# An attention and SwiGLU training kernel: weight gradients on 20 full row tiles, with transposes moved between TensorE and the DMA crossbar

## The chip, the cores and the metric

The kernel runs on one core of a Trainium2 chip. The metric is device time in microseconds (us) for one launch, the median of several runs. A core has TensorE (matrix products, results in PSUM), VectorE, ScalarE and GpSimd for work on tiles, SyncE, which here only issues DMAs, and 16 DMA engines that all queues share. Each engine runs its instructions in order; DMAs are issued from SyncE's queue (SP), ScalarE's and GpSimd's. A transposing DMA ("crossbar transpose") turns rows into columns on the way into SBUF.

## The reference

The launch computes the output and all gradients of a block on x of 2048 rows by 640, in bf16:

```
xn  = layernorm(x)
s   = memory attention over 64 segments of 32 rows, one after the other:
        h = [mem (8 rows); xn segment (32 rows)]        40 rows
        q, k, v = h Wq, h Wk, h Wv                      32 heads of 128
        p = softmax(mask(q k^T / sqrt(128)))
        o = (p v) Wo;  mem = o[first 8 rows];  s rows = o[last 32 rows]
g   = silu( (silu(xn w1) * (xn w3)) w2 )                F = 1728
out = x + s * g
gradients of x, mem0, Wq, Wk, Wv, Wo, w1, w3, w2 for a given grad_out
```

Because each segment's memory comes from the one before, h has 2048 + 64 x 8 = 2560 rows in all: 2048 x rows and 512 memory rows.

## The kernel before

The stages follow each other: layer norm and SwiGLU forward (to about 450 us), attention forward, attention backward (the chain over segments, to 3394 us), weight gradients (`phase6_Awgrads`, 3394 to 4905), the gradient of Wo (`phase6b_gWo`, to 5085) and SwiGLU backward with the layer norm's (`phase5_Bbwd_ln`, to 5535).

Attention works on tiles `tl` of three segments, 22 in all: 21 with 120 rows (24 memory rows first, then 96 x rows) and one of 40. `geo(tl)` gives segments, memory rows nm, x rows nx and all rows n. Probabilities P and score gradients dS of a tile are stored in DRAM as `PR[tl]` and `DSR[tl]`, n rows by 32 heads by n columns; inputs and row gradients lie in stores that `x_src`, `m_src` and `g_src` address.

The weight-gradient stage takes eight blocks `qd` of 4 heads (512 columns) and in each the 22 tiles; a unit `u` is one tile in one block. For each unit:

- `ld` loads dS, P and three row tiles `r6` (the gradient of o, q and k): four loads on SP for dS, P and the x rows of q and k, one on ScalarE's queue, the memory rows on GpSimd's.
- `s1` transposes dS on TensorE (4 heads, L1333) and VectorE copies it out (L1335).
- `s2` makes the rows' gradients of v, k and q (L1345, 12 products), which ScalarE and VectorE copy to `gr` (L1348 to L1352); 22 tiles stay for the whole block.
- `s3` transposes `gr` on TensorE (12 products, L1364), and copies put it into `ring`, a cyclic buffer of 384 rows.
- `s4` multiplies each complete window of 128 rows of the ring by the transposed weights (L1381, 24 products) and adds it to `ghacc`, the gradient of h (L1388, L1390). It does so for all 2560 rows, 20 windows, although only x rows are read later.

After the 22 units, `wg` makes the three weight gradients of the block (L1403): for each, 5 sums over the 22 tiles, and stores them through SP (L1408). `ld_w` loads the block's weights by crossbar transposes, and the generator `head` puts the first units of the next block between the three `wg`. `in_order` ties the instructions of the stage on every engine to the written order, so no engine takes a later unit's instruction first.

`turned_load` (L280) issues a crossbar transpose on SP. Besides the weights, the SwiGLU backward uses it for gz (16 transposes), for ggT (112) and for `GU`, the stored up gradient. Its matrix products are `pghb` (L1757), `pgxb` (L1773), `w2a` (L1726) and `wa` (L1809). This stage is not held to the written order.

Of the kernel before, what the change touches and what calls it, by code (L numbers as in the profile page):

```python
# [16 lines left out]
P = 128  # L17
# [23 lines left out]
class K:  # L41
# [76 lines left out]
    def build_masks(self, pool, scr):  # L118
        nc = self.nc
        GE = ALU.is_ge  # L120
        n, nm = 120, 24
# [7 lines left out]
        for (c0, w) in ((0, 8), (nm, 32)):  # L129
            v1 = a1[:, c0:c0 + 3 * w].rearrange("p (s c) -> p s c", c=w)  # L130
            v2 = a2[:, c0:c0 + 3 * w].rearrange("p (s c) -> p s c", c=w)
            sel(v1, 1, 0, [[-8, 3], [0, w]])
            sel(v1, -1, 7, [[8, 3], [0, w]])
            sel(v2, 1, -nm, [[-32, 3], [0 if w == 8 else -1, w]])
            sel(v2, -1, nm + 31, [[32, 3], [0, w]])
# [8 lines left out]
        sel(b1[:], -1, 7, [[0, 40]])  # L144
        sel(b2[:], 1, 0, [[-1, 40]])
# [6 lines left out]
    def setup_dram(self):  # L152
# [17 lines left out]
        self.GXA = mk("GXA", (self.NR, D))  # L170
# [23 lines left out]
        for tl in range(self.NTL):  # L194
            n = self.geo(tl)[3]
            self.PR.append(mk(f"PR{tl}", (n, H, n)))
            self.DSR.append(mk(f"DSR{tl}", (n, H, n)))
            ns, nm = self.geo(tl)[0:2]
            self.VTD.append(mk(f"VTD{tl}", (P, ns, H, 40)))
        self.PM = mk("PM", (T, P, 80))  # L200

# [25 lines left out]
    def m_src(self, tl, w, c0, c1):  # L227
        g = c0 // 1024
        out, t = [], 3 * tl
        end = t + self.geo(tl)[0]  # L230
        while t < end:
            e = min(end, t - t % 4 + 4)
            XS = self.store(w)[t // 4, g, 0:8, t % 4:t % 4 + e - t]
            for i in range(2 if w == "qv" else 1):
                X = XS[:, :, i] if w == "qv" else XS
                out.append((8 * (t - 3 * tl), 8 * (e - 3 * tl), X[:, :, c0 - 1024 * g:c1 - 1024 * g].rearrange("r t c -> t r c"), i))
# [8 lines left out]
    def m_rows(self, A, t):  # L245
        r = 120 * (t // 3) + 8 * (t % 3)
        return A[r:r + 8, :]

    def x_rows(self, A, X, eng):
        n = self.NTL - 1  # L250
        eng.dma_start(A[0:120 * n, :].rearrange("(t r) d -> t r d", r=120)[:, 24:120],
                      X[0:96 * n, :].rearrange("(t r) d -> t r d", r=96))
        eng.dma_start(A[120 * n + 8:self.NR, :], X[96 * n:self.S, :])


    def x_pieces(self, A, x0, x1):
        out, a = [], x0
        while a < x1:
            tl = a // 96
            b = min(x1, 96 * tl + 96)  # L260
            r = 120 * tl + self.geo(tl)[1] + a - 96 * tl
            out.append((a - x0, b - x0, A[r:r + b - a, :]))
            a = b
        return out
# [103 lines left out]
def phase3_Afwd(k, W4, Wv, Wk_):  # L368
# [30 lines left out]
    with tc.tile_pool(name="ast", bufs=1) as st, tc.tile_pool(name="achain", bufs=1) as ch, \  # L399
# [174 lines left out]
        def ld(w, tl, qd, eng=nc.sync):  # L574
# [4 lines left out]
            k.load_x(r, nm, k.x_src(tl, w, c0, c0 + 512), eng)  # L579
# [11 lines left out]
        def scores(tl, qd):  # L591
# [8 lines left out]
            for j in range(4):  # L600
                kv = kT[:, h0 + j, 0:n].rearrange("p (s c) -> p s c", c=40)
                nc.tensor.matmul(sp[:, j, 0:nm], qT[:, j, :], kv[:, :, 0:8], start=False, stop=True,
                                 skip_group_check=True)
                nc.tensor.matmul(sp[:, j, nm:n], qT[:, j, :], kv[:, :, 8:40], start=False, stop=True,
# [19 lines left out]
        def norm(tl, qd, eng=nc.gpsimd, q=nc.gpsimd):  # L624
# [6 lines left out]
            q.dma_start(k.PR[tl][:, h0:h0 + 4, :], Pb[0:n, :, 0:n])  # L631
# [19 lines left out]
        def pv(tl, qd, q=nc.gpsimd):  # L651
# [3 lines left out]
            if 4 * tl < k.NO:  # L655
                pt = ps.tile([P, 4, 96], F32, name="xot", tag="x", bufs=5)
                for j in range(4):
                    nc.tensor.matmul(pt[:, j, :], v[0:n, j * P:(j + 1) * P], PTs[qd % 2][0:n, j, 24:120], start=True, stop=True)
# [126 lines left out]
def phase3b_out(k, Wo, W0, W4):  # L785
# [12 lines left out]
    with tc.tile_pool(name="oio", bufs=1) as io, tc.tile_pool(name="oac", bufs=1, space=bass.MemoryType.PSUM) as pa, \  # L798
# [6 lines left out]
        def ld(b, qd):  # L805
# [3 lines left out]
            if nt == 3:  # L809
                src = k.OR[120 * tl:120 * tl + 360, c0:c0 + 512].rearrange("(t r) c -> r t c", r=120)[24:120]  # L810
            else:
                nm, n = k.geo(tl)[1], k.geo(tl)[3]
                src = k.OR[120 * tl + nm:120 * tl + n, c0:c0 + 512].rearrange("(t r) c -> r t c", t=1)
# [82 lines left out]
        while g0:  # L896
# [6 lines left out]
    later = [(k.GWO[0:120 * n, :].rearrange("(t r) d -> t r d", r=120)[:, 24:120], k.GS[0:96 * n, :].rearrange("(t r) d -> t r d", r=96)),  # L903
             (k.GWO[120 * n + 8:k.NR, :], k.GS[96 * n:k.S, :])]

    for s in range(3):
# [3 lines left out]
        for b in range(2):  # L910
            r0 = 120 * tl0 + 8 * s
            dst = k.HRO[120 * tl0:120 * tl0 + 120 * (n - 1), :].rearrange("(t r) d -> t r d", r=120)[:, 8 * s:8 * s + 8]
            r1 = 120 * (tl0 + n - 1) + 8 * s
# [3 lines left out]
            later.append((k.HRO[r1:r1 + 8, cols], k.FS[t1, 32 * b:32 * b + 8, :]))  # L917
# [6 lines left out]
def phase4_Abwd(k, out2, WoT, WvT, WkT, WqT, later):  # L924
# [3 lines left out]
    with tc.tile_pool(name="gst", bufs=1) as st, tc.tile_pool(name="gchain", bufs=1) as ch, \  # L928
# [6 lines left out]
        bdf = st.tile([P, 16, 8], BF16, name="bdf")  # L935
# [338 lines left out]
def phase6_Awgrads(k, X, out0, out3, out4, out5):  # L1274
# [6 lines left out]
    R = 384  # L1281
# [618 lines left out]
```

## Time and profile before

| what | us |
|---|---|
| median of 3 runs | 5541.81 (5536.53 to 5544.77) |
| profiled execution, its own time | 5536.53 |
| its span, first to last instruction | 5534.8 |
| TensorE busy in the span | 4889.1 (88%) |
| VectorE, ScalarE, GpSimd busy | 2323.4, 1746.8, 1583.1 |
| weight-gradient stage, 3394 to 4905 | TensorE busy 1410.89 of 1511, granted clock 0.96, DMA share 0.44 |
| w2 gradient, 5085 to 5175 | TensorE busy 68.95 of 90 |
| SwiGLU backward with layer norm, 5175 to 5412 | TensorE busy 208.38 of 237, VectorE 125.28, DMA share 0.73 |
| w1 and w3 gradients, 5412 to 5535 | TensorE busy 117.33 of 123 |

All but the first row are of one profiled execution. Matmuls are pipelined, so their listed durations overlap and a busy engine can still take more. A queue's instructions (SPq) are listed with the time that they hold the queue, not with the time to landing.

### The profile page before, as it was taken

The page shows a single profiled execution, that of the slowest core. Times are in us where ns is not written, and L with a number is a line of the kernel's source. Part 1 is how long each engine was busy: PE and PEld are TensorE (multiplying, and loading weights), DVE is VectorE, ACT ScalarE, POOL GpSimd, SP SyncE. Part 2 cuts the span into 40 slices and gives each one's busy share as a digit, 9 for nine tenths or more (in the row PEclk, how much of TensorE's full clock was granted, in tenths as well). Part 3 has the DMA queues.
Part 4 walks back from the last instruction along what each step waited for, and adds up shares of the span by engine and source line. Part 5 has one row for each costly group of instructions (what it writes and reads, how often), then busy time and mean ns, then how long its engine had stood idle before and what let it go on. Part 6 is the DMA issues. An engine that isn't in the chain of part 4 may idle for free. (4 is left out here: it accounts for less than half of the span.)

```text
span 5534.8 us, 164066 instructions
## 1 busy us (share of the span) xinstructions
PE 4889.1 (88%) x66145; PEld 3115.9 (56%) x66492; DVE 2323.4 (42%) x7358; ACT 1746.8 (32%) x4913; POOL 1583.1 (29%) x2620
## 2 busy tenths in 40 slices
PE   4987888888888676989999996999999999998899
PEld 2544555555555444656666664566566556656555
DVE  5833555555555323444444542233223323311351
ACT  2422555555555322323333331232223222300000
POOL 0000344444444212333333333243224323310110
PEclk9998999999999787999999998999999999999999
DMA  7553455555555686666766665354335334548573
GB/s 251 172 186 90 138 158 151 156 151 161 153 149 143 147 178 148 181 187 183 191 183 182 185 175 124 89 122 102 83 89 122 93 84 97 130 163 226 130 161 95
DMA packets 1193943, 817.94 MB, mean 148 GB/s; under 512 B 742603, under 2 KB 1086311, under 8 KB 1190507
## 3 DMA queue, kind: packets, MB, share of 16 engines
q1 hardware_dynamic: 952451, 564.78, 39.1%
q0 software_dynamic: 93520, 151.54, 9.8%
q10 hardware_dynamic: 147212, 91.09, 6.5%
q8 instruction: 525, 8.60, 0.7%
q14 instruction: 235, 1.93, 0.1%
HBM read 461.39 MB, written 296.78 MB: 137 GB/s over the span
## 5 line engine op out<-in xcount | busy, mean ns | idle before, releaser
L1403 PE MATMUL wg<-gr,hr 120*128 120x512 bf16 (+1 forms) x2640 | 591.1, 385 | 17.3 <-DVE dST L1335 13.1
L1381 PE MATMUL g<-w,gT 128*128 128x320 bf16 x3840 | 549.9, 300 | 0.0
L1403 PEld LDWEIGHTS <-hr 120*128 120x128 bf16 (+1 forms) x2640 | 258.3, 99 | 342.0 <-issue 50.1
L1381 PEld LDWEIGHTS <-gT 128*128 128x128 bf16 x3840 | 369.3, 98 | 137.4
L243 POOL DMA_DIRECT2D r<-GOS x256 | 143.3, 564 | 796.2 <-PE r6p L1345 706.5
L90 DVE CAST wgo<-wg 128x512 bf16<-128x512 f32 x72 | 47.5, 688 | 585.9 <-issue 280.2
L316 PEld LDWEIGHTS <-hx 128*32 128x32 bf16 x7680 | 180.4, 98 | 169.7 <-issue 13.7
L90 DVE CAST stg<-bank 128x512 bf16<-128x512 f32 x256 | 177.1, 692 | 209.2 <-PE bank L316 199.6
L335 PEld LDWEIGHTS <-gkv 128*8 128x8 bf16 x8192 | 190.0, 87 | 105.7 <-DVE gkv L1012 24.2
L619 ACT ACTIVATE xP<-xsp,xnm 120x120 bf16<-120x120 f32 (+1 forms) x704 | 239.9, 375 | 8.8 <-DVE xnm L615 5.0
L1390 DVE TENSOR_TENSOR ghacc<-ghacc,g 128x320 f32<-128x320 f32 x240 | 117.2, 488 | 277.6 <-PE g L1381 277.6
L92 ACT CAST wgo<-wg 128x512 bf16<-128x512 f32 x48 | 25.8, 589 | 638.6 <-PE wg L1403 638.6
L1163 POOL DMA_DIRECT2D DSR<-gdS x176 | 101.5, 577 | 429.5 <-DVE gdS L1161 384.1
L1348 ACT CAST gr<-r6p 120x512 bf16<-120x512 f32 (+1 forms) x176 | 103.1, 586 | 362.4 <-PE r6p L1345 340.7
L668 POOL DMA_DIRECT2D OR<-xv x163 | 94.5, 580 | 420.0 <-ACT xv L667 304.1
L92 ACT COPY gT<-t6g 128x960 bf16<-128x960 bf16 (+5 forms) x216 | 166.9, 792 | 120.2 <-PE t6g L1364 117.4
L630 POOL TENSOR_TENSOR xP<-xP,xrz 120x480 bf16<-120x480 bf16 x163 | 161.7, 992 | 141.1 <-ACT xP L619 96.5
L1161 DVE SCALAR_TENSOR_TENSOR gdS<-gdp,Dx,gPr 120x120 bf16<-120x120 f32 (+1 forms) x680 | 182.8, 330 | 0.0
L1232 PE MATMUL gbank<-WqT,ident 128*128 128x512 bf16 x453 | 158.0, 398 | 20.0 <-issue 12.3
L1364 PE MATMUL t6g<-ident,gr 120*128 120x120 bf16 (+1 forms) x2112 | 172.0, 221 | 3.3 <-DVE wgo L90 2.7
L316 PE MATMUL gbank<-WoT,gox 128*32 128x512 bf16 x2560 | 153.7, 387 | 23.8 <-POOL gox L967 20.5
L335 PE MATMUL bank<-Wo,oTm 128*32 128x320 bf16 x4032 | 172.6, 324 | 0.1
(329 smaller groups left out, 10835.2 us busy)
## 6 DMA issues: line engine op xcount, KB each, us to landing
QVS<-stg SPq DMA_DIRECT2D x128, 256.0 KB
gqv<-QVS SPq DMA_DIRECT2D x108, 192.0 KB
vTt<-VTD SPq DMA_DIRECT2D x64, 320.0 KB
VTD<-gvT POOLq DMA_DIRECT2D x168, 120.0 KB, 3.7
OR<-xv POOLq DMA_DIRECT2D x163, 120.0 KB, 2.5
DSR<-gdS POOLq DMA_DIRECT2D x168, 112.5 KB, 3.4
dS<-DSR SPq DMA_DIRECT2D x168, 112.5 KB
P<-PR SPq DMA_DIRECT2D x168, 112.5 KB
```

Source lines behind the costliest of these rows:

```text
L90: return nc.vector.tensor_copy(out, in_)
L92: return nc.scalar.copy(out, in_)
L243: eng.dma_start(d, src if src.shape[0] > 1 else src[0])
L316: k.nc.tensor.matmul(bank[32 * g:32 * g + 32, :], x[:, dc, :], W[:, dc, c0:c0 + 512], start=(dc == 0), stop=(dc == k.DC - 1), tile_positio ...
L335: k.nc.tensor.matmul(pm[p0:p0 + nq, 0:320], x[:, h, :], W[:, h, 320 * b:320 * b + 320], start=(first and i == 0), stop=(last and i == 15), ...
L619: nc.scalar.activation(Pb[0:n, j, 0:n], sp[0:n, j, :], ACT.Exp, bias=nmx[0:n, j:j + 1], scale=k.scale, accum_out=Z[0:n, j:j + 1])
L630: eng.tensor_tensor(Pb[0:n, :, 0:n], Pb[0:n, :, 0:n], bc_last(rz[0:n], n), ALU.mult)
L1161: nc.vector.scalar_tensor_tensor(dS[0:n, j, :], dp[0:n, j, :], Dx[0:n, j:j + 1], Pr[0:n, j, :], op0=ALU.subtract, op1=ALU.mult)
L1232: nc.tensor.matmul((bA if g in ("W1", "G1", "G2") else bB)[:], k.ident[:], WqT[:, 0, 0:512], start=True, stop=True)
L1364: nc.tensor.transpose(pt[:, i - i0, j, :], st["g", u, i][0:n, j * P:(j + 1) * P], k.ident[0:n, 0:n])
L1381: nc.tensor.matmul(pg[:], ring[:, i, j, r0:r0 + P], Ws[qd][i][:, j, 320 * h:320 * h + 320], start=(i == 0 and j == 0), stop=(i == 2 and j ...
L1403: nc.tensor.matmul(accs[dc][:], hr[0:n, tl, dc * P:(dc + 1) * P], st["g", NTL * qd + tl, i][0:n, :], start=(tl == 0), stop=(tl == NTL - 1))
```

## The change

- In every tile x rows now come first and memory rows last; masks, slices and stores follow. P and dS are stored with 128 columns per head in place of n, the unused ones zero.
- The ring and the products of `s4` take x rows alone: 16 windows instead of 20. Two partial tiles (`NF` = 20 and 21) come first in each block and have ring rows of their own.
- `wg` sums over 20 tiles of 128 rows: the 160 rows of the two partial tiles go to DRAM (`GSP`) and come back as rows 120 to 127 of the 20 full tiles (`spill`). `hr` is loaded in the same way.
- dS is transposed by a crossbar transpose (`dturn`), and so are the x rows of `gr` into the ring (`s3`): four per unit on SP in place of 16 TensorE transposes and their copies. Loads run 5 units ahead.
- In the SwiGLU backward it is the other way: gz, ggT and guT are transposed on TensorE and copied out of PSUM, with fewer PSUM buffers for the products; `GU` is stored by rows and loaded plainly. The gradient of h (`GXA`) has only x rows and is loaded with one DMA per 128 rows.

```diff
-        self.GXA = mk("GXA", (self.NR, D))
+        self.GXA = mk("GXA", (S, D))
         self.HRO = mk("HRO", (self.NR, D))
...
-            self.PR.append(mk(f"PR{tl}", (n, H, n)))
-            self.DSR.append(mk(f"DSR{tl}", (n, H, n)))
+            self.PR.append(mk(f"PR{tl}", (n, H, P)))
+            self.DSR.append(mk(f"DSR{tl}", (n, H, P)))
             ns, nm = self.geo(tl)[0:2]
...
+        self.GSP = mk("GSP", (8, 3, 160, 512))
 
     def x_src(self, tl, w, c0, c1):
...
             eng.tensor_tensor(Pb[0:n, :, 0:n], Pb[0:n, :, 0:n], bc_last(rz[0:n], n), ALU.mult)
-            q.dma_start(k.PR[tl][:, h0:h0 + 4, :], Pb[0:n, :, 0:n])
+            q.dma_start(k.PR[tl][:, h0:h0 + 4, :], Pb[0:n])
 
...
     NW = k.NR // P
+    NF = NTL - 2
+    NS = k.NR - 120 * NF
     R = 384
+    NB = 5
+    assert NS == 8 * NF and NW == NF and (96 * NF) % R == 0 and S - 96 * NF == P
+    order = [NF, NF + 1] + list(range(NF))
...
         start = len(nc.cur_bb.bb.instructions)
-        hr = hp.tile([120, NTL, D], BF16, name="hr")
-        acc = X.tile([P, NW, D], F32, name="ghacc", tag="x")
-        NB = 3
-        dSs = [hp.tile([120, 4, P], BF16, name=f"dS6{i}") for i in range(NB)]
+        hr = hp.tile([P, NF, D], BF16, name="hr")
+        grs = [hp.tile([P, NF, 512], BF16, name=f"gr{i}") for i in range(3)]
+        xt = X.tile([P, NT * D + 3 * 2 * (R + P)], F32, name="ghacc", tag="x")
+        acc = xt[:, 0:NT * D].rearrange("p (w d) -> p w d", d=D)
+        ring = xt[:, NT * D:].bitcast(BF16).rearrange("p (i j c) -> p i j c", i=3, j=4)
...
+        units = [(qd, tl) for qd in range(8) for tl in order]
+        st, Ws, cnt = {}, {}, dict(w=0, s=0, g=0, l=0)
...
-            nc.sync.dma_start(dS[0:n, :, 0:n], k.DSR[tl][:, h0:h0 + 4, :])
-            nc.sync.dma_start(Pr[0:n, :, 0:n], k.PR[tl][:, h0:h0 + 4, :])
+            nc.sync.dma_start(dS[0:n], k.DSR[tl][:, h0:h0 + 4, :])
+            nc.sync.dma_start(Pr[0:n], k.PR[tl][:, h0:h0 + 4, :])
...
-        def s1(u):
+        def ld_to(u):
+            while cnt["l"] < min(u, len(units)):
+                ld(cnt["l"])
+                cnt["l"] += 1
+
+        def dturn(u):
+            if u >= len(units):
+                return
+            dST = io.tile([P, 4, P], BF16, name="dST6", tag="dST6", bufs=4)
+            turned_load(k, dST[:], st["l", u][0][:].rearrange("p j c -> p (j c)"))
+            st["d", u] = dST
+
+        def s2(u):
             qd, tl = units[u]
             n = k.geo(tl)[3]
-            dS = st["l", u][0]
-            pt = pa.tile([P, 4, n], BF16, name="t6", tag=bank("x", 5, 3))
-            for j in range(4):
-                nc.tensor.transpose(pt[:, j, :], dS[0:n, j, :], k.ident[0:n, 0:n])
-            dST = dSTs[u % 2]
-            nc.vector.tensor_copy(dST[0:n, :, 0:n], pt[0:n])
-
...
+            dS, Pr, rw = st.pop(("l", u))
+            lhs = (Pr, dS, st.pop(("d", u)))
+            st["g", u] = []
+            for i in range(3):
+                pr = pa.tile([P, 512], F32, name="r6p", tag=bank("s", 3, 5))
+                for j in range(4):
+                    nc.tensor.matmul(pr[:, j * P:(j + 1) * P], lhs[i][0:n, j, :], rw[i][0:n, j * P:(j + 1) * P],
+                                     start=True, stop=True)
+                if tl < NF:
+                    gr = grs[i][:, tl, :]
+                else:
+                    gr = gp.tile([120, 512], BF16, name="grs", tag=f"grs{i}", bufs=2)[:]
+                if i == 0:
+                    nc.scalar.copy(gr[0:n], pr[0:n])
+                elif i == 1:
+                    nc.vector.tensor_scalar(gr[0:n], pr[0:n], k.scale, None, op0=ALU.mult)
+                else:
+                    nc.scalar.activation(gr[0:n], pr[0:n], ACT.Copy, scale=k.scale)
+                st["g", u].append(gr)
+                if tl >= NF:
+                    r0 = 120 * (tl - NF)
+                    nc.gpsimd.dma_start(k.GSP[qd, i, r0:r0 + n, :], gr[0:n])
+
+        def spill(qd):
+            for i in range(3):
+                nc.gpsimd.dma_start(grs[i][120:P, :, :], k.GSP[qd, i].rearrange("(t r) c -> r t c", r=8))
+
+        def s3(u):
...
-        def s3(u, i0, i1):
-            qd, tl = units[u]
-            n = k.geo(tl)[3]
-            c = i1 - i0
-            pt = pa.tile([P, c, 4, n], BF16, name="t6g", tag=bank("x", 5, 3))
-            for i in range(i0, i1):
-                for j in range(4):
-                    nc.tensor.transpose(pt[:, i - i0, j, :], st["g", u, i][0:n, j * P:(j + 1) * P], k.ident[0:n, 0:n])
-            a = (120 * tl) % R
-            b = min(n, R - a)
-            for (p0, p1, d0) in ((0, b, a), (b, n, 0)):
-                if p1 > p0:
-                    k.copy(ring[:, i0:i1, :, d0:d0 + p1 - p0], pt[:, :, :, p0:p1], eng='s' if c == 2 else 'v')
+            ns, nm, nx, n = k.geo(tl)
+            a = (96 * tl) % R if tl < NF else R + 96 * (tl - NF)
+            b = min(nx, R - a) if tl < NF else nx
+            for i, gr in enumerate(st.pop(("g", u))):
+                for (p0, p1, d0) in ((0, b, a), (b, nx, 0)):
+                    if p1 > p0:
+                        turned_load(k, ring[:, i, :, d0:d0 + p1 - p0], gr[p0:p1, :])
 
         def s4(u):
             qd, tl = units[u]
-            n = k.geo(tl)[3]
-            for w in range((120 * tl) // P, (120 * tl + n) // P):
-                r0 = P * (w % 3)
+            if tl < NF:
+                ws = [(w, P * (w % 3)) for w in range((96 * tl) // P, (96 * tl + 96) // P)]
+            else:
+                ws = [(NT - 1, R)] if tl == NF + 1 else []
+            for w, r0 in ws:
...
-            for tl in range(NTL):
-                n = k.geo(tl)[3]
+            for tl in range(NF):
                 for dc in range(DC):
-                    nc.tensor.matmul(accs[dc][:], hr[0:n, tl, dc * P:(dc + 1) * P], st["g", NTL * qd + tl, i][0:n, :],
-                                     start=(tl == 0), stop=(tl == NTL - 1))
+                    nc.tensor.matmul(accs[dc][:], hr[:, tl, dc * P:(dc + 1) * P], grs[i][:, tl, :],
+                                     start=(tl == 0), stop=(tl == NF - 1))
...
-        ld(0)
+        def head(u0):
+            s2(u0)
+            yield
+            s2(u0 + 1)
+            ld_to(u0 + 1 + NB)
+            s3(u0)
+            yield
+            s2(u0 + 2)
+            ld_to(u0 + 2 + NB)
+            s3(u0 + 1)
+            yield
+
+        ld_to(3)
+        dturn(0)
         ld_w(0)
-        ld(1)
-        ld(2)
-        def head(u0):
-            s1(u0)
-            yield
-            for i in range(3):
-                s2(u0, i)
-            s1(u0 + 1)
-            yield
-            s3(u0, 0, 2)
-            s3(u0, 2, 3)
-            ld(u0 + 3)
-            for i in range(3):
-                s2(u0 + 1, i)
-            s1(u0 + 2)
-            yield
+        ld_to(4)
+        dturn(1)
+        nc.scalar.dma_start(hr[0:120], k.HRO[0:120 * NF, :].rearrange("(t p) d -> p t d", p=120))
+        nc.scalar.dma_start(hr[120:P], k.HRO[120 * NF:k.NR, :].rearrange("(t r) d -> r t d", r=8))
+        dturn(2)
+        ld_to(5)
+        dturn(3)
         for _ in head(0):
             pass
         for qd in range(8):
             u0 = NTL * qd
-            for tl in range(NTL):
-                u = u0 + tl
-
-                if tl + 4 < NTL:
-                    ld(u + 4)
-                if tl + 2 < NTL:
-                    s2(u + 2, 0)
-                    s2(u + 2, 1)
-                if tl + 3 < NTL:
-                    s1(u + 3)
-                if tl + 1 < NTL:
-                    s3(u + 1, 0, 2)
-                if tl + 2 < NTL:
-                    s2(u + 2, 2)
-                if tl + 1 < NTL:
-                    s3(u + 1, 2, 3)
+            for p in range(NTL):
+                u = u0 + p
+                if p + 3 < NTL:
+                    s2(u + 3)
+                    ld_to(u + 3 + NB)
+                dturn(u + 4)
+                if p + 2 < NTL:
+                    s3(u + 2)
                 s4(u)
-                if tl % 11 == 2:
-                    out_ld(2 * qd + tl // 11)
-                if tl % 11 == 6:
-                    out_rows(2 * qd + tl // 11)
+                if p == 4:
+                    spill(qd)
+                if p % 11 == 2:
+                    out_ld(2 * qd + p // 11)
+                if p % 11 == 6:
+                    out_rows(2 * qd + p // 11)
             if qd < 7:
                 ld_w(qd + 1)
                 h = head(u0 + NTL)
-                for i in range(3):
-                    ld(u0 + NTL + i)
...
-    GU = k.dp.tile([F, S], BF16, name="GU", uniquify=False)
+    GU = k.dp.tile([S, F], BF16, name="GU", uniquify=False)
...
                     for tt in range(NT):
-                        turned_load(k, gzT[:, :, tt * P:(tt + 1) * P], gz[:, tt, :])
+                        pt = psA.tile([P, DC, P], BF16, name="gzp", tag="gzp")
+                        for dc in range(DC):
+                            nc.tensor.transpose(pt[:, dc, :], gz[:, tt, dc * P:(dc + 1) * P], k.ident[:])
+                        k.copy(gzT[:, :, tt * P:(tt + 1) * P], pt[:], eng='vs'[tt % 2])
...
-                        tc.tile_pool(name="c5pc", bufs=4, space=bass.MemoryType.PSUM) as psC, \
-                        tc.tile_pool(name="c5pd", bufs=2, space=bass.MemoryType.PSUM) as psD:
+                        tc.tile_pool(name="c5pc", bufs=2, space=bass.MemoryType.PSUM) as psC, \
+                        tc.tile_pool(name="c5pd", bufs=1, space=bass.MemoryType.PSUM) as psD:
...
-                                turned_load(k, ggtok[:, b0 // P:b0 // P + 2, fc * P:fc * P + fsz], ggT[0:fsz, fc, :])
-                        nc.gpsimd.dma_start(GU[0:FR, cols].rearrange("(c p) t -> p c t", p=P), guT[:, 0:FC - 1, :])
-                        nc.gpsimd.dma_start(GU[FR:F, cols], guT[0:F - FR, FC - 1, :])
...
+                            gut = bp.tile([P, F], BF16, name="gutok", tag="gutok")
+                            for i, (gT, dst) in enumerate(((ggT, ggtok[:, tt, :]), (guT, gut[:]))):
+                                pt = psC.tile([P, 2 * 1024], BF16, name="ptt5", tag="ptt5", bufs=2)
+                                for fc in range(FC):
+                                    fsz = fszs[fc]
+                                    nc.tensor.transpose(pt[:, fc * P:fc * P + fsz], gT[0:fsz, fc, tcol], k.ident[0:fsz, 0:fsz])
+                                nc.vector.tensor_copy(dst[:, 0:704], pt[:, 0:704])
+                                nc.scalar.copy(dst[:, 704:F], pt[:, 704:F])
+                            nc.sync.dma_start(GU[rows, :], gut[:])
...
-                            k.load_x(gar, 0, k.x_pieces(k.GXA, tt * P, tt * P + P), nc.scalar)
+                            nc.scalar.dma_start(gar[:], k.GXA[rows, :])
...
-                for f in range(4):
-                    turned_load(k, gutok[:, :, 432 * f:432 * f + 432], GU[432 * f:432 * f + 432, :])
+                for t0 in range(0, NT, 2):
+                    nc.scalar.dma_start(gutok[:, t0:t0 + 2, :], GU[t0 * P:(t0 + 2) * P, :].rearrange("(t p) f -> p t f", p=P))
```

## The prediction

> **What bounds the kernel now.** I read the groups of instructions first, then busy time by window, to find the stages and what limits each in the part that the change rewrites. The weight-gradient stage runs from 3394 to 4905 us of the 5534.8 us span, in eight periods, one per column block `qd` of 512. The window view has one period; columns are length, busy time of TensorE, weight load, VectorE, ScalarE and GpSimd, then granted clock, DMA share and GB/s:
>
> ```profile
> 3609.90:3716.60 106.70, 101.38 (x1077) 81.11 (x1078) 50.66 (x113) 43.86 (x70) 55.77 (x101) 0.97 0.55 127
> 3530.30:3609.90 79.60, 75.32 (x352) 33.33 (x352) 5.98 (x11) 3.86 (x8) 1.70 (x3) 0.98 0.24 59
> ```
>
> The first row is the loop over the 22 units, the second the three `wg` sums with the head of the next block: 186.3 us together, TensorE busy for 95%. The chain that ended last shows one unit:
>
> ```profile
> 4559.95 0.10 PE t L1333 x2
> 4560.05 0.42 PE t6g L1364 x8
> 4560.47 0.22 PE r6p L1345 x4
> 4560.70 0.21 PE t6g L1364 x4
> 4560.91 3.26 PE g L1381 x24
> 4564.17 0.45 PE r6p L1345 x8
> 4564.62 0.21 PE t L1333 x4
> ```
>
> Nothing but TensorE, a new unit every 4.77 us: 0.83 us are transposes (L1333, L1364), 0.67 us the rows' gradients (L1345), 3.26 us the window products (L1381). So an instruction with 128 columns costs 0.055 us in the stream and one with 320 costs 0.136, less than the listed means, which overlap. The sync queue has room here (start, length, instruction):
>
> ```profile
> 3650.02 0.34 SPq L1316 DMA_DIRECT2D dS<-DSR  x1
> 3650.45 0.44 SPq L1317 DMA_DIRECT2D P<-PR  x1
> 3650.99 0.40 SPq L275 DMA_DIRECT2D r<-QVS  x1
> 3651.56 0.32 SPq L275 DMA_DIRECT2D r<-KS  x1
> 3654.79 0.34 SPq L1316 DMA_DIRECT2D dS<-DSR  x1
> ```
>
> Four loads take 1.9 us of the queue, then it waits for TensorE until 3654.79. The last view is the price of a transpose on that queue: of line 280 (the helper `turned_load`) durations min/median/max in ns, then one row of the timeline:
>
> ```profile
> L280 SPq DMA_TRANSPOSE ggtok<-ggT x112: 1167/1197/3370, 5177.4 to 5402.4; - x112
> L280 SPq DMA_TRANSPOSE x<-gz_all x16: 1199/1276/1287, 5113.2 to 5133.1; - x16
> ...
> 5113.15 21.26 SPq L280 DMA_TRANSPOSE x<-gz_all  x16
> ```
>
> A transpose from SBUF holds the queue for about 1.2 us whether it turns 128x256 (64 KiB) or 128x640 (160 KiB), and the next one starts only after it: 16 of them fill 21.26 us, 1.33 each.
>
> [...] here four L1345 products take 0.63 us after the stage's first stalls and 0.39 later.
>
> **The change, part by part.**
>
> *Removed from TensorE in the unit loop.* 16 transposes, 16 x 0.055 = 0.88 us per unit; with x rows only, 16 windows instead of 20, so 4 x 24 x 0.136 = 13.1 us per block. Left in the loop: 19 units' products (3 lie in the head), 19 x 0.67 = 12.7, and 16 x 3.26 = 52.2, 65 us in place of about 101. ScalarE and VectorE lose the copies of turned rows (20.9 us of ScalarE in that window); both were waiting for TensorE.
>
> *Removed from `wg`.* 20 tiles instead of 22: 300 products x 0.216 us (110 took 23.4 to 24.5 us) = 64.7 instead of 71.2. With two short head steps and bank stalls I take 69 us for 79.6.
>
> *Added to the sync queue.* Per unit one transpose of dS (128x512) and three of gradients (96x512), all inside measured shapes. Unloaded I take 1.30 us each, between the 1.29 pitch of 128x256 and 1.33. DMA share: 416 KiB of transposes per unit at the 0.61 share and 119 GB/s of the gz run's last part is about 2.2 us of all engines, and the loads some 2.4 (0.51 of 4.77), 4.6 per 7 us. At 0.73 to 0.78, in the ggT stage, a few transposes stretched to 2 to 3 us. I add 3%: 1.34. Ends: 1.26 and 1.6.
>
> *The queue sets the loop.* `in_order` fixes each engine's order. Iterations p = 0 to 18 hold four loads (1.9), one dS transpose and three gradient transposes; p = 19 has no load. That is 19 x 1.9 + 80 x 1.34 = 143.3 us against TensorE's 65. The queue cannot work ahead: `s3(u+2)` waits for products of the previous iteration, and TensorE cannot start `wg` before the last `s4`, which waits for the last `s3`. Each gradient transpose waits for a ScalarE or VectorE copy of the previous iteration and for the ring's slot, last read by `s4(u-1)`; behind it in the queue stand the next unit's loads and dS transpose, and TensorE's products wait for those. A dS transpose waits for a load issued three iterations earlier, which has long landed. So all these waits are short while the queue is the slower side; on a faster queue they would hand the time back to TensorE. During `wg` the queue carries only 3 weight transposes, 15 stores, 3 units' loads and 6 gradient transposes, and mostly waits.
>
> *Edges.* After the third `wg` come five stores (3.0 us before, 3794.4 to 3797.4), a load (1.9) and three transposes (3.9) before p = 0: 8.8. At the end the last transpose lands some 2 us after issue (stores in the chain land in 1.6 to 2.3), then 24 products[...]: 4.8.
>
> Block: 8.8 + 143.3 + 2 + 4.8 + 69 = 227.9 us against 186.3: +41.6. Eight: +333. The last loop of before was 7 us longer than the others, so -7; filling the pipeline with dS transposes +4; in the last block 16 GXA stores now stand in the bound queue, each behind its `s4`, 16 x 0.4 = +6. Stage: **+336 us**.
>
> *SwiGLU backward.* The 16 gz transposes leave SP (21.3 us); instead 80 on TensorE, 4.4 us, with one PSUM bank. Uncovered, each bank turn adds about 1 us, 16 in all. The earlier 15.8 us stall of TensorE came from ScalarE, whose queue sat behind the w1/w3 transposes, which stay; some 4 us of late stores go. From -16 to +20: I take 0. The 112 ggT transposes go; 448 TensorE transposes come, 24.6 us, onto 208 busy of 237. Copies (704 columns on VectorE, 1024 on ScalarE) are hidden: VectorE had 125 us busy, ScalarE 12. With fewer PSUM buffers they run beside the next block's products; uncovered, 16 x 1 us. In return the waits for `du` and `sl` (27.3 and 13.0 us on VectorE, 28 on TensorE) should about halve. From -5 to +35: I take +10. GU written by rows and reloaded from ScalarE's queue hides under the first 58 us of L1809, as the 28 us of GU transposes did.
>
> *Attention stages.* Order of rows, masks and fixed dS tiles leave products and shapes as they are. Padding P and dS to 128 columns makes their rows 1 KiB runs instead of 240 bytes; GpSimd's P store (848 ns against 580 for OR) gets cheaper, but TensorE waits there on fsum, Pm and PTm. From -20 to +10: I take -5. The two spills and reload of the partial tiles ride on GpSimd, 9 DMAs x 0.57 = 5 us per block, with some 100 us to spare.
>
> Sum: 336 + 0 + 10 - 5 = +341. On the profiled execution's 5536.53 us that is 5878; the median of the three runs, 5541.81, is 5 us above that execution, so about **5880 us**.
>
> **Rivals.**
>
> *TensorE stays the bound, and the kernel is faster.* For: half a period's TensorE work per unit goes, and loads were fully hidden. It decides at one price: the loop breaks even at 143.3 - 41.6 = 101.7 us, (101.7 - 36.1) / 80 = 0.82 us per transpose. Below some 0.4 a block would take 69 + 65 + 6 = 140, -46 x 8 = -370 us, about 5180; at 0.7 each it takes about 175, some 5450. Against: of 128 transposes from SBUF none was below 1.167.
>
> *The crossbar and loads choke each other.* The first 14 ggT transposes took 28.23 us, 2.0 each, with the DMA share at 1. At 1.6 each the loop grows by 80 x 0.26 = 21 us: +166, about 6050. Against: only at full share, partly waiting for data; 4.6 of 7 us leaves a third free.
>
> *The queue's work hides under `wg`.* Total queue work is 88 x 1.34 + 22 x 1.9 + 8 + 6 = 174 us per block, less than 186; spread evenly the stage would be 100 us shorter than before. Against: the written order, as above. A half-success, 20 us less per block, gives 5720.
>
> **How the numbers follow.** Queue-bound as worked out: 84%, 5790 to 5975. Choked: 7%. Half hidden: 4%. Faster: 5%, within no change almost none. From the likeliest I leave some 5% at each end, so low 5760, high 5990. About 0.2% is what a measurement of this kernel tells from no change: faster 0.05, same 0.01, slower 0.94.
>
> **What would show it.** Right: the loop at 140 to 150 us with TensorE under half busy, waiting for gradient transposes, SP issuing back to back at 1.3 us; `wg` near 69. Wrong: transposes of 96x512 issued in well under 1 us, or the loop at TensorE's 65 us; or the ggT stage, not this one, carrying the loss.

## The result

| | median (us) | from | to | runs |
|---|---|---|---|---|
| before | 5543.29 | 5536.53 | 5554.52 | 4 |
| after | 5991.96 | 5976.29 | 6008.43 | 4 |

The change makes the kernel slower by 8.1%: ratio 1.0808, 95% interval 1.0771 to 1.0845. The forecast was 5880 us, with a range up to 5990; the result lies 112 us above the one and 2 us above the other. The side and what bounds the loop were as foretold; the size was short.

The profiled execution of after is the slowest of its four (6008.43 us, span 6006.7) and that of before the fastest, so the two profiles differ by 472 us, and the medians by 449.

Busy time by window, one period of the stage as before: the loop over the units, then the three `wg` (length, busy TensorE, weight load, VectorE, ScalarE, GpSimd, granted clock, DMA share, GB/s).

```profile
3941.40:4106.69 165.29, 91.03 (x620) 60.19 (x618) 30.94 (x57) 23.37 (x41) 52.76 (x95) 0.77 0.69 141
3869.87:3941.40 71.53, 66.92 (x328) 31.00 (x332) 6.65 (x11) 4.97 (x10) 9.77 (x18) 1.00 0.34 76
```

The loop has grown from 106.70 to 165.29 us, with TensorE busy for 55% of it in place of 95%. `wg` has shrunk from 79.60 to 71.53. The sync queue shows why the loop has grown, in one unit of the timeline (start, length):

```profile
4019.48 3.81 SPq L272 DMA_TRANSPOSE ghacc<-gr  x3
4023.38 0.54 SPq L1312 DMA_DIRECT2D dS<-DSR  x1
4023.97 0.40 SPq L1313 DMA_DIRECT2D P<-PR  x1
4024.46 0.33 SPq L267 DMA_DIRECT2D r<-QVS  x1
4024.96 0.31 SPq L267 DMA_DIRECT2D r<-KS  x1
4025.33 1.20 SPq L272 DMA_TRANSPOSE dST<-dS  x1
4026.63 3.79 SPq L272 DMA_TRANSPOSE ghacc<-gr  x3
```

Three gradient transposes, four loads, one dS transpose, and at 4026.63 the next unit: 7.15 us with no gap over 0.2. Before, the queue paused 2.9 us in each unit of 4.8. The transposes themselves, among all those that line 272 issues from 3640 us to the end of the stage (durations min/median/max in ns):

```profile
L272 SPq DMA_TRANSPOSE ghacc<-gr x420: 1179/1197/2602, 3718.4 to 5286.7; - x140
L272 SPq DMA_TRANSPOSE dST<-dS x150: 1194/1198/2265, 3717.1 to 5274.4; - x150
```

The waits of TensorE between 3640 and 5290 us (total, times, longest) put it under another name:

```profile
PE r6p L1344 <- DMA dST<-dS: 485.0, 108, 13.1
PE g L1387 <- DMA ghacc<-gr: 24.3, 37, 2.1
```

Read alone, these say that TensorE waits for a transfer to land. The transfer lands late because its instruction stands behind seven others in the queue; whether the queue or the landing sets the pace is what the experiments had to tell.

Stage by stage the profiles differ like this; the second column is the prediction's own sum, split at the same places and rounded. The first row ends with the last product of `gdp`, the gradient of P in the attention stage; the last steps of attention, another 79 us before and 81 after, fall in the second row.

| stretch | foretold | profile |
|---|---|---|
| up to the last product of `gdp` | -5 | +20.2 |
| from there to the first `wg` (215.5 to 296.9) | +56 | +81.4 |
| seven periods, `wg` to `wg` (186.6 to 237.1 each) | +290 | +353.3 |
| last `wg` (74.6 to 67.7) | -11 | -6.9 |
| gradient of Wo, w2 | 0 | +0.4 |
| SwiGLU backward (238.3 to 260.3) | +10 | +22.0 |
| w1 and w3 gradients | 0 | +1.7 |
| sum | +341 | +472 |

The first row is in large part scatter between executions. The last product of `gdp` ends at 3314.8 us before and at 3335.0 after; in the ten profiles of the study with after's attention stages it ends between 3311 (`e10_hr_later`) and 3338 (`e1_no_spill`), 3327 in the mean. Whether the changed attention stages cost some 12 us, one profile of before cannot tell.

### The profile page after: what moved, and what is told of

It reads as the page before. It is cut to its first block, busy times and chain, and to the rows that moved or that the text cites. A ratio compares the mean times of both kernels' runs of the same rounds, so it can differ in the third digit from the quotient of the medians.

```text
span 6006.7 us, 157450 instructions
## 1 busy us (share of the span) xinstructions
PE 4808.6 (80%) x62801; PEld 2969.6 (49%) x63196; DVE 2184.3 (36%) x6934; ACT 1628.5 (27%) x4737; POOL 1557.7 (26%) x2675
## 5 line engine op out<-in xcount | busy, mean ns | idle before, releaser
L1387 PE MATMUL g<-w,ghacc 128*128 128x320 bf16 x3072 | 592.1, 363 | 26.7 <-DMA ghacc<-gr 26.6
L1344 PE MATMUL r6p<-r,dST 120*128 120x128 bf16 (+1 forms) x704 | 85.6, 258 | 590.0 <-DMA dST<-dS 570.8
L1408 PE MATMUL wg<-gr,hr 128*128 128x512 bf16 x2352 | 525.3, 382 | 19.3 <-DVE grs L1353 13.3
L1387 PEld LDWEIGHTS <-ghacc 128*128 128x128 bf16 x3072 | 356.0, 119 | 235.5 <-DMA ghacc<-gr 43.2
L1408 PEld LDWEIGHTS <-hr 128*128 128x128 bf16 x2400 | 235.6, 98 | 302.0 <-issue 27.3
L1396 DVE TENSOR_TENSOR ghacc<-ghacc,g 128x320 f32<-128x320 f32 x192 | 93.7, 488 | 755.8 <-PE g L1387 755.8
L1344 PEld LDWEIGHTS <-dST 120*128 120x128 bf16 (+1 forms) x704 | 51.2, 112 | 613.7 <-DMA dST<-dS 604.5
L1351 ACT CAST gr<-r6p 120x512 bf16<-120x512 f32 x160 | 93.8, 586 | 559.2 <-PE r6p L1344 379.9
L245 POOL DMA_DIRECT2D r<-KS x256 | 140.7, 552 | 359.9 <-PE r6p L1344 305.7
L1355 ACT ACTIVATE gr<-r6p 120x512 bf16<-120x512 f32 x160 | 95.8, 599 | 449.1 <-PE r6p L1344 448.7
```

The lines of the kernel that those rows point to most:

```text
L245: eng.dma_start(d, src if src.shape[0] > 1 else src[0])
L1344: nc.tensor.matmul(pr[:, j * P:(j + 1) * P], lhs[i][0:n, j, :], rw[i][0:n, j * P:(j + 1) * P], start=True, stop=True)
L1387: nc.tensor.matmul(pg[:], ring[:, i, j, r0:r0 + P], Ws[qd][i][:, j, 320 * h:320 * h + 320], start=(i == 0 and j == 0), stop=(i == 2 and j ...
L1408: nc.tensor.matmul(accs[dc][:], hr[:, tl, dc * P:(dc + 1) * P], grs[i][:, tl, :], start=(tl == 0), stop=(tl == NF - 1))
```

## The experiments

Each kernel stands beside runs of the kernel before on the same chip. Those had a median of 5554.04 in the group of the first four, 5547.23 in that of the second four, 5540.50 in that of the last two, and 5543.29 beside after. So a difference of some 10 us between kernels of two groups shows nothing by itself.

| kernel | median (us) | ratio to before | 95% interval |
|---|---|---|---|
| after | 5991.96 | 1.0808 | 1.0771 to 1.0845 |
| e1_no_spill | 5958.48 | 1.0735 | 1.0706 to 1.0765 |
| e2_loads_actq | 5898.65 | 1.0636 | 1.0606 to 1.0667 |
| e3_old_swiglu | 5972.79 | 1.0767 | 1.0743 to 1.0791 |
| e4_turn_tensor | 5571.76 | 1.0036 | 1.0019 to 1.0052 |
| e5_ds_tensor | 5799.20 | 1.0453 | 1.0424 to 1.0483 |
| e6_all_tensor | 5471.02 | 0.9864 | 0.9840 to 0.9889 |
| e7_all_tensor_mix | 5405.93 | 0.9738 | 0.9709 to 0.9766 |
| e8_spread | 5968.07 | 1.0764 | 1.0735 to 1.0793 |
| e9_no_pad | 6040.78 | 1.0903 | 1.0885 to 1.0922 |
| e10_hr_later | 5977.44 | 1.0792 | 1.0771 to 1.0814 |

The theory: the sync queue sets the loop, by the number and length of the instructions in it. Its rivals: the transfers choke each other in the DMA engines, or single transfers (the spill, the loads at the stage's start) hold everything up.

### The sync queue: loads moved, transposes moved

**e2_loads_actq** issues two of the four loads on ScalarE's queue.

```diff
-            nc.sync.dma_start(dS[0:n], k.DSR[tl][:, h0:h0 + 4, :])
-            nc.sync.dma_start(Pr[0:n], k.PR[tl][:, h0:h0 + 4, :])
+            nc.scalar.dma_start(dS[0:n], k.DSR[tl][:, h0:h0 + 4, :])
+            nc.scalar.dma_start(Pr[0:n], k.PR[tl][:, h0:h0 + 4, :])
```

> The two loads of dS and P of each unit are issued on ScalarE's queue in place of SP; bytes, transposes and order stay. Theory (SP's issue time sets the loop): an iteration loses 0.53 + 0.44 us of queue and the gaps beside them, 7.1 falls to about 6.1, 19 x 1.0 x 8 = 150 us less, about 5840. Rival (the DMA engines, 0.69 to 0.72 busy in the loop, or the crossbar are the bound): the iteration stays at 7.1, within 20 us of 5992. Second rival (ScalarE's row copies get stuck behind its loads): slower than 5992.

Measured 5898.65: 93 us less, where the theory expected 150, and its rival at most 20. The same bytes move and the same transposes are made; only two issues of 0.4 to 0.55 us per unit have left the queue. Its timeline:

```profile
4002.02 3.81 SPq L272 DMA_TRANSPOSE ghacc<-gr  x3
4005.94 0.52 SPq L267 DMA_DIRECT2D r<-QVS  x1
4006.56 0.36 SPq L267 DMA_DIRECT2D r<-KS  x1
4006.97 1.19 SPq L272 DMA_TRANSPOSE dST<-dS  x1
4008.27 3.84 SPq L272 DMA_TRANSPOSE ghacc<-gr  x3
```

The undisturbed unit takes 6.25 us, 0.90 less, near the 1.0 expected. Not every unit is undisturbed: the mean loop fell by 14.1 us (164.9 to 150.8), not by the 17 that 19 such units make, and in four of the seven loops between two `wg` phases the dS transposes held the queue for 1392 to 1456 ns in the mean, where after has 1203 to 1256 in all seven. The queue's occupancy is the bound; some of what is taken off it comes back as longer transposes.

**e5_ds_tensor** turns dS on TensorE, as before, and leaves the gradients on the crossbar: one transpose of four leaves the queue.

```diff
-            turned_load(k, dST[:], st["l", u][0][:].rearrange("p j c -> p (j c)"))
...
+            for j in range(4):
+                nc.tensor.transpose(pt[:, j, :], dS[0:n, j, :], k.ident[0:n, 0:n])
...
+            nc.vector.tensor_copy(dST[0:n, :, 0:n], pt[0:n])
```

> The changed kernel, but dS is turned on TensorE, as before; the gradients of rows stay on the crossbar. Takes 22 of 85 to 88 transposes per column block off the sync queue. Theory 'the sync queue sets the loop': some 20 of them lie in the loop, at 1.23 us and a gap of 0.06 each 26 us per block, 206 in eight: 5785 us, between 5765 and 5830; a typical iteration goes from 7.15 to 5.85 us. Rival 'the transfers choke each other, so that late landings and not the queue set the pace': the loop keeps more than half of that time, 5880 us or more.

Measured 5799.20, 193 us less. Two units' starts in its timeline:

```profile
3955.80 3.78 SPq L272 DMA_TRANSPOSE ghacc<-gr  x3
...
3961.69 3.79 SPq L272 DMA_TRANSPOSE ghacc<-gr  x3
```

5.89 us per unit, 1.26 less than after. The mean loop is 140.8 us, 24.1 less, and eight times that is the 193. Under the rival, late landings, the kernel would have taken 5880 us or more.

**e4_turn_tensor** does the opposite: gradients on TensorE (x rows alone), dS on the crossbar. In the loop:

```diff
-        def s3(u):
...
-                        turned_load(k, ring[:, i, :, d0:d0 + p1 - p0], gr[p0:p1, :])
+        def s3(u, i0, i1):
...
+                for j in range(4):
+                    nc.tensor.transpose(pt[:, i - i0, j, :], st["g", u][i][0:nx, j * P:(j + 1) * P], k.ident[0:nx, 0:nx])
...
+            k.copy(ring[:, i0:i1, :, d0:d0 + nx], pt[:], eng='s' if c == 2 else 'v')
```

> The changed kernel with the three gradients of a unit transposed on TensorE again and copied into the ring by ScalarE and VectorE, x rows only; dS still goes through the crossbar, and row order, 16 windows, 20 full tiles and spills stay. SP then holds 1.9 + 1.3 us per unit. Theory (SP-bound loop): TensorE sets the loop again, 19 x (0.67 + 0.66) + 16 x 3.26 = 77 us plus some 5 at the edges and the reload's 7 partly hidden, 154 to 161 per block in place of 237, 610 to 660 less, 5330 to 5390, below the kernel before as well. Rival (the loop is held by the loads' and spills' DMA traffic, not by SP): a loop of 120 us or more, above 5650.

Measured 5571.76: 420 us come back, but the 5330 to 5390 foretold was missed by 182; the rival's figure, above 5650, was not reached either. The sync queue is no longer full (66 us busy in a loop of 107.9, the mean of the first six between two `wg` phases), so something else sets the pace. Its loop by window, and the longest of TensorE's waits from 3550 to 4740 us:

```profile
3807.90:3912.08 104.18, 85.08 (x876) 65.84 (x876) 38.27 (x78) 37.87 (x62) 52.91 (x95) 0.90 0.89 166
```

```profile
PE r6p L1348 <- DMA dST<-dS: 109.1, 33, 10.5
```

The DMA share is 0.89, and TensorE still waits for dS transposes. The seventh and last of these loops takes 135.1 us. In this block the stores of `GXA` stand in the sync queue, where they wait for VectorE's sums for 63.6 us (15 waits), and the dS transposes stand behind them.

**e6_all_tensor** therefore combines e4 and e5: no crossbar transpose is left in the loop but those of the weights. The PSUM banks are shared out anew: two for the rows' gradients and three for the transposed tiles, where e4 has three and two.

> The kernel with the gradients of rows turned on TensorE, and now dS on TensorE too, so that no crossbar transpose is left in the loop except the weights'. That kernel took 5572 us, some 180 us more than TensorE's work in it explains. Theory 'with the queue free, the DMA engines are full (share 0.87 to 0.92 in its loop), and the dS transposes are what fills them': the loop falls from some 106 us to about 90, 5440 us, at most 5500. Rival 'loads, the partial tiles' spill and the start of the stage take that time, the dS transposes little': 5540 to 5575.

Measured 5471.02, 101 us below e4 and 1.4% below the kernel before. Its loop:

```profile
3796.50:3892.48 95.98, 86.77 (x966) 69.62 (x964) 45.37 (x101) 38.27 (x63) 52.98 (x95) 0.96 0.65 151
```

The share falls to 0.65, TensorE is busy for 90%, and no wait for the landing of a dS transpose is left. So in e4 the dS transposes were the bound. The seven loops gain 95 us, 35 of them in the last one. Whether the dS transposes held e4 up through the DMA engines' occupancy or through their landing time (they are issued one unit ahead, and a unit takes some 4 us there) these runs do not tell apart.

e6 is also the change without the crossbar transposes that it brought into the loop. x rows alone and 20 full tiles are worth 1.4% with the new SwiGLU backward included; the crossbar transposes turn that into a loss of 8.1%.

### What was costed at nothing: the spill

**e1_no_spill** leaves the 160 rows of the two partial tiles out of the weight gradients, and with them their way through DRAM. The rows 120 to 127 of the full tiles are zero instead.

```diff
-                    nc.gpsimd.dma_start(k.GSP[qd, i, r0:r0 + n, :], gr[0:n])
...
-                if p == 4:
-                    spill(qd)
```

> Leaves out the 160 rows of the two partial tiles in the three weight gradients: nothing is stored to GSP, spill does not run, rows 120 to 127 of the gradient tiles stay zero. All else is the changed kernel. Theory (the reload of 20 x 8 rows into only eight partitions takes 10.6 us to land and holds the dS transposes up behind it, once per block): the one iteration per block that now takes 10 to 16 us falls to 7 to 8, 8 x 7 = 56 us less, about 5935. Rival (the long iteration comes from the loop filling up, whatever the reload does): no iteration changes, 5975 to 5995.

Measured 5958.48: 33 us less, between theory and rival. In the trace the loop falls from 164.9 to 159.0 us in the mean, and in the first six of seven loops no unit takes over 9 us from one dS transpose to the next. What the spill does is seen in after's timeline of the queues, around its three loads at 3970.93:

```profile
3970.93 1.85 POOL L1363 DMA_DIRECT2D gr<-GSP  x3
```

```profile
3972.33 0.57 SPq L1312 DMA_DIRECT2D dS<-DSR  x1
3972.95 0.40 SPq L1313 DMA_DIRECT2D P<-PR  x1
3973.45 2.77 SPq L267 DMA_DIRECT2D r<-QVS  x1
3976.32 0.36 SPq L267 DMA_DIRECT2D r<-KS  x1
3976.74 1.21 SPq L272 DMA_TRANSPOSE dST<-dS  x1
3980.53 5.42 SPq L272 DMA_TRANSPOSE ghacc<-gr  x3
```

A load of 0.33 us holds the queue for 2.77, three transposes of 3.8 for 5.42, and between 3977.95 and 3980.53 the queue stands still. From 3968 to 3980 the DMA share is 0.94; GpSimd's queue alone takes 0.57 of the engines' time, and its bytes there are nearly all the spill's. One unit of each block takes 11 to 16.5 us in place of 7.15. The three transfers need long to land (us, min/median/max):

```profile
DMA to landing us min/median/max: 7.2/10.6/13.6
```

The last of the three lands 12.1 to 14.8 us after the first is issued, so their 480 KiB move at 33 to 41 GB/s in the mean. No run here varies the number of partitions, so whether the eight that they go into are the reason is not shown.

**e8_spread** keeps the spill, one transfer at the 5th, 10th and 15th unit.

```diff
...
-                if p == 4:
-                    spill(qd)
+                if p in (4, 9, 14):
+                    spill(qd, (p - 4) // 5)
```

> The changed kernel with its spill spread: one of the three transfers at the 5th, 10th and 15th unit of a block in place of all three at the 5th. Leaving the partial tiles' rows out altogether had given 5958. Theory 'the three transfers hold the DMA engines as one burst of 12 us, which nothing else can cover': spread they hide in an iteration of 7 us each, and 25 to 35 us of it come back, 5957 to 5967. Rival 'the cost is their sum, wherever they stand': 5985 or more.

Measured 5968.07, 24 us less, a microsecond past the burst theory's end, and the mean loop is 160.9, 3.9 less of the 5.8 that leaving it out gives. The interval of the ratio overlaps with that of after, so the loop has to decide: the burst is the cause of the larger part of the price, which goes when it is spread. Each transfer now lands in 5.4 to 8.8 us.

### The smaller terms

**e3_old_swiglu** puts the SwiGLU backward of before back (`phase5_Bbwd_ln` whole, reading the smaller `GXA` in one load per 128 rows).

> The changed kernel with the SwiGLU backward stage of before (crossbar transposes of gz, ggT and the stored up gradient, four and two PSUM buffers), only the gradient of h is loaded in its new layout. Theory (the stage's 448 TensorE transposes and scarcer PSUM cost more than the shorter DMA waits give): from the traces, 22 us less, about 5970. Rival (the stage is neutral and its 22 us are drift of the profiled executions): within 8 us of 5992.

Measured 5972.79, 19 us less of the 22 expected. In the trace the stage takes 239.7 us in place of 260.3. The two versions by window, before and then after:

```profile
5175.00:5413.30 238.30, 208.75 (x1456) 136.71 (x1457) 126.10 (x315) 12.44 (x30) 40.50 (x39) 0.96 0.73 159
```

```profile
5623.30:5883.60 260.30, 240.18 (x1904) 164.13 (x1905) 145.28 (x352) 43.07 (x64) 26.22 (x23) 0.99 0.38 117
```

TensorE has 31.4 us more to do with 448 transposes, 0.070 each where 0.055 had been taken, and is idle for 20.1 us in place of 29.6. The copies are hidden, as foretold, but for some 4 us of waits.

**e9_no_pad** takes the padding of P and dS away, in DRAM, in the stores and in every load; the loads of this stage:

```diff
-            nc.sync.dma_start(dS[0:n], k.DSR[tl][:, h0:h0 + 4, :])
-            nc.sync.dma_start(Pr[0:n], k.PR[tl][:, h0:h0 + 4, :])
+            nc.sync.dma_start(dS[0:n, :, 0:n], k.DSR[tl][:, h0:h0 + 4, :])
+            nc.sync.dma_start(Pr[0:n, :, 0:n], k.PR[tl][:, h0:h0 + 4, :])
```

> The changed kernel with P and dS stored and loaded without the padding to 128 columns, as before: runs of 240 bytes in place of whole rows of 1 KiB. Theory 'the sync queue sets the loop, by the number of its instructions': within 15 us of the changed kernel's 5992. Rival 'the padding is what keeps the DMA engines free for the transposes (share 0.69 in the loop)': 6030 or more.

Measured 6040.78, 49 us more. The queue theory missed it, and the number is the rival's. In the loop the DMA engines are indeed busier (share 0.75 in the second loop, where after has 0.69), but that costs little time there: an undisturbed unit takes 7.3 us in place of 7.15, the load of P holding the queue for 0.47 us in place of 0.40, and the mean period grew by only 2.0 us (237.1 to 239.0). The profiled execution as a whole grew by 19 (span 6025.6): it is the fastest of its kernel's four, that of after the slowest. Its last `gdp` product ends at 3345.6 us, later than in all ten profiles with the padding, so some of the price may lie in the attention stages. In all, runs of 240 bytes in place of whole rows cost 0.8% of the kernel (49 of 5992 us). Most of the 49 us cannot be placed from one profile.

**e10_hr_later** moves the last 8 partitions of `hr` out of the stage's start.

```diff
-        nc.scalar.dma_start(hr[120:P], k.HRO[120 * NF:k.NR, :].rearrange("(t r) d -> r t d", r=8))
...
+                if u == 7:
+                    nc.gpsimd.dma_start(hr[120:P], k.HRO[120 * NF:k.NR, :].rearrange("(t r) d -> r t d", r=8))
```

> The changed kernel with the last 8 partitions of hr loaded from GpSimd's queue in the eighth unit of the first block, not ahead of the stage's first units. The first block took some 25 us more than the others with what was allowed for filling. Theory 'this transfer into 8 partitions holds up the first loads and dS transposes (the sync queue waited 17.8 us for it)': 12 to 20 us come back, 5972 to 5980. Rival 'the five units' own loads fill that time': within 6 us of 5992.

Measured 5977.44, within the range of the theory, but by luck. From the last `gdp` product to the first `wg` it takes 295.4 us in place of 296.9, and to the first window product 144.8 in place of 149.2. Of the 31 us between the two profiles 24 lie ahead of that, where the kernels are the same. The theory falls: this transfer costs some 2 to 4 us.

### A version faster than both

**e7_all_tensor_mix** is e6 with the SwiGLU backward of before, the spill spread, and `hr` loaded later.

> As the kernel with all transposes of the loop on TensorE, with three more edits: the SwiGLU backward of before (19 us less when it was put back alone), the spill of the partial tiles as one transfer each at the 5th, 10th and 15th unit of a block in place of three at the 5th, and the last 8 partitions of hr loaded during the first block rather than before it. If these three add up: 19 + 8 x 4 + 10, some 60 us under that kernel, 5380 to 5440. If the spill's stall only moves to three places: 20 to 30 us under it.

Measured 5405.93, 65 us under e6: the edits add up. Against the kernel before it is 2.6% faster (0.9738, 0.9709 to 0.9766), with a mean loop of 94.1 us where before had 107.3.

## Why the prediction was right or wrong

*What bounds the loop: right.* The sum made the loop 158.9 us; with the spill left out it takes 159.0. So close a match is partly luck: the unit was put at 7.26 us and takes 7.15 (a transpose at 1.34 and takes 1.27 with its gap), so 19 units are 2 us shorter than foretold and the edges as much longer. In after's mean loop the queue's instructions take 143.5 us and the gaps of under 0.2 us between them another 14.7, together 158 of 164.9. (The forecast's 143.3 counts those gaps and leaves out the edges, so it is not the same figure.) e5 and e2 show the slope: what leaves the queue leaves the time. The signs named for being right came only in part: the loop takes 165 us and not 140 to 150, TensorE is busy for 55% of it and not under half, and its waits are for the dS transposes (485 us) far more than for those of the gradients (24 us). That TensorE stays the bound, that the crossbar chokes at 1.6 us each, and that the work hides under `wg` are all refuted: TensorE is busy for 55% of the loop, a transpose holds the queue for 1.20 us in the median, and the loop takes 165 us.

*The spill: wrong.* The step that failed is the prediction's "The two spills and reload of the partial tiles ride on GpSimd, 9 DMAs x 0.57 = 5 us per block, with some 100 us to spare". It priced the issuing engine and not the transfer: three transfers into 8 partitions that take most of the DMA engines' time for some 12 us (0.57 of it from 3968 to 3980) and hold up the queue that sets the loop. The spill costs 5.8 us per loop, 47 in eight by the loops of the trace, 33 by the medians. This one step is more than the 2 us by which the result passes the range, but it is not the whole of the 112; the rest are the terms below.

*Filling the pipeline: mis-sized.* +4 was taken; from the last `gdp` product to the first window product it takes 149.2 us in place of 120.4, +29, of which 2 belong to the end of attention. Kernels without dS transposes on the crossbar take 134 to 138, so some 12 us are these. The `hr` transfer is not the rest; the five units' loads ahead of the loop remain, untested.

*`wg`: mis-sized.* The sums alone were right: the last `wg`, with no head steps between, takes 64.9 us for the 64.7 foretold. With the head the phase takes 72.2 us in the mean for 69. TensorE waits there for bank and gradient copies (20.8 us for `wgo` copies and 13.3 for `grs` in the stage). Over seven such phases that is some 22 us.

*SwiGLU backward: direction right, 12 us short.* The transposes cost 31 us and not 24.6, and TensorE's idle time fell by 9.5 us, where halving its 28 us of waits would have given 14. That is 7 us and 5. The w2 gradient, costed at 0, changed by -1.5. The 1 us for each turn of a PSUM bank was the author's estimate; for the bank of the gz transposes (`gzp`) TensorE waited in after 13.3 us in two waits, one of them 12.8.

*Attention, -5: not seen.* The scatter of 27 us between profiles with the same attention stages is larger than the term. GpSimd's store of P did get shorter with the padding: 559 ns in the median, in place of 845 before and 842 in `e9_no_pad`. The +6 for the stores of `GXA` is borne out: in after's last loop a unit takes 7.64 us in the median, 0.49 more than elsewhere.

Together (42 us from seven loops, 22 from seven `wg` and 4 from the last, 25 from the start, 12 from SwiGLU, 25 ahead of the stage with the -5) these make 130 of the 131 us by which the profiles' difference passes the sum. The median passes the forecast by 112, less because the profiled execution was the slowest of its four.

## What to carry to other kernels

Price a DMA twice: by what it holds on the queue that issues it, and by what it does to the others' transfers until it has landed: the spill's three loads took 1.85 us of GpSimd, which had time to spare, and the loop is 5.8 us shorter without the spill. When a stage moves from an engine to a queue, count every instruction of that queue per unit, plain loads too, and test the claim by taking one of them off the queue with the same bytes moved. A change with a useful and a harmful half is best judged in halves: here the smaller ring and full tiles, with all else of the change, gain 1.4% once no transpose of dS or of the gradients stands in the queue.

## What was not expected of the hardware

- A crossbar transpose of dS held the queue for 1.2 us whether the queue was busy for some 60% of the loop or for nearly all of it (medians 1199 ns in e4 and 1198 in after), but the cost on the DMA side did not add up: the 22 dS transposes of a loop go with a DMA share of 0.89 in 104 us (e4) against 0.65 in 96 us without them (e6), while 85 transposes of dS and gradients in 165 us go with 0.69 (after).
- Plain loads held the sync queue for 0.31 to 0.54 us each, four of them for a quarter of the unit, and up to 2.77 us while the spill was in flight.
- With TensorE idle for 45% of the loop its granted clock was 0.77, against 0.97 before. In that window the products left in the loop, which the forecast put at 65 us, took 91.03: the 24 of one group between 3.42 and 6.19 us (L1387, 3955 to 4085), where before every such group took 3.42 or 3.43 (L1381, 3650 to 3700). What this costs was not tested.
